# Keeping weight loads and x loads out of the way of the DMA transposes at the start of a fused attention and FFN kernel

## Chip, cores, metric

One core of a Trainium2 chip runs the whole program. The metric is the device time in microseconds (us) of one execution. A profile's span is about 2.3 us shorter than the time of the same execution, so spans are compared with spans and times with times.

## The reference

A pre-norm transformer block in bf16 with 2048 tokens and D = 1024. Attention has 32 query heads of 32 and one shared K and V head. The FFN is 3584 wide.

```python
x = A_x
h = x + attention(layernorm(x), wq, wk, wv, wo)      # 32 heads, one K and one V head
n = layernorm(h)
out = h + (sigmoid(n @ w_gate) * (n @ w_up)) @ w_down
```

## The kernel before

The program is written out by a planner in Python. The planner simulates the engines, fixes the order of instructions on each of them, and adds the waits. On the chip, every engine and every queue then follows its own list in that order. So a wrong guess of a landing time in the planner does not change the result; it leaves an engine waiting.

The start concerns us. x comes in 16 tiles of 128 tokens. VectorE (DVE) normalises each tile in place. Then the tile has to be transposed ("turned") before K, V and Q can be computed from it. Tiles 0 and 1 are turned on TensorE (PE), tiles 2 to 15 by transposing DMAs from SP's queue:

```python
def dma_xT(t):
    xT_ev[t] = dma(lambda: SP.dma_start_transpose(
        out=xnT4[t // 4][:, :, (t % 4) * P:(t % 4 + 1) * P], in_=x_sb[:, t, :]), f"xT{t}", P * D * 5 // 2,
        [xnorm[t]], prio=0, occ=1330.0)
```

The x loads of tiles 8 to 15 go out in pairs from ACT's queue, each after an earlier tile is normalised, and the weight pieces are paced so that the planner's picture of the DMA stays short:

```python
if 1 < ts[-1] < NT - 6:
    load_x([ts[-1] + 5, ts[-1] + 6], [xnorm[ts[-1]]], "act")
# ...
def pump(t):
    while paced and t >= next_piece[0] and pl.dma_free["sp"] < t + (2500.0 if NT - 1 in xT_ev and known([xT_ev[NT - 1]], t) else 600.0):
        # ... issue the next piece of w_o, w_gate, w_up or w_down on SP's queue
```

Scores are computed in "visits" (one pair of exponentials on ACT each). The first 16 visits need K of tiles 0 to 7 only; the following ones need the later tiles. `KNOBS` is a list of planning choices, one tuple for each 8 visits, which a search had picked for this kernel.

The softmax here doesn't subtract the row's maximum and nothing guards it: scores larger than these inputs give would overflow.

## Time and profile before

| | kernel before |
|---|---|
| timed executions | 1083.32 us median of 3 (1081.85 to 1084.2) |
| profiled execution | 1086.84 us, span 1084.6 us |
| ACT busy | 1006.7 us, of it 970.6 us in 1024 exponentials |
| PE busy | 1045.1 us |
| last exponential ends | 1004.06 + 14.97 = 1019.0 us |
| from there to the end | 65.6 us, matmuls |

### The profile page before, as it was taken

The page shows a single profiled execution, that of the slowest core. Times are in us where ns is not written, and L with a number is a line of the kernel's source. Part 1 is how long each engine was busy: PE and PEld are TensorE (multiplying, and loading weights), DVE is VectorE, ACT ScalarE, POOL GpSimd, SP SyncE. Part 2 cuts the span into 40 slices and gives each one's busy share as a digit, 9 for nine tenths or more (in the row PEclk, how much of TensorE's full clock was granted, in tenths as well). Part 3 has the DMA queues.
Part 4 walks back from the last instruction along what each step waited for, and adds up shares of the span by engine and source line. Part 5 has one row for each costly group of instructions (what it writes and reads, how often), then busy time and mean ns, then how long its engine had stood idle before and what let it go on. Part 6 is the DMA issues. An engine that isn't in the chain of part 4 may idle for free.

```text
span 1084.6 us, 31397 instructions
## 1 busy us (share of the span) xinstructions
PE 1045.1 (96%) x12801; PEld 482.2 (44%) x12970; DVE 903.9 (83%) x1757; ACT 1006.7 (93%) x1165; POOL 29.4 (3%) x58
## 2 busy tenths in 40 slices
PE   8899999999999999999999999999999999999998
PEld 6654444444444444444444444444444444444443
DVE  8779989898888889898898989898898989898721
ACT  6889999999999999999999999999999999999610
POOL 2100000000000000000000000000000000000000
PEclk9999999999999999999999999999999999999999
DMA  9986698956969496979569498977959596976994
GB/s 226 229 268 209 178 266 222 268 140 187 261 153 276 128 226 159 258 206 281 157 144 251 140 252 166 248 205 190 251 136 245 143 275 161 238 190 166 270 272 114
DMA packets 309359, 226.60 MB, mean 209 GB/s; under 512 B 121824, under 2 KB 300512, under 8 KB 309216
## 3 DMA queue, kind: packets, MB, share of 16 engines
q1 hardware_dynamic: 306048, 222.37, 80.0%
q10 hardware_dynamic: 3168, 2.23, 0.8%
q8 instruction: 102, 1.67, 0.6%
q14 instruction: 41, 0.34, 0.1%
HBM read 194.12 MB, written 7.86 MB: 186 GB/s over the span
## 4 chain that ended last, share of the span: by engine, by line
PE 65%; ACT 19%; DVE 7%; issue 6%; DMA 2%; POOL 0%; DVEq 0%
PE F_ps L401 54%; ACT Pr L693 17%; PE S_ps L401 11%; DVE Ts L727 2%; ACT tnh L968 2%; DMA zone<-ring 1%; DVE st L338 1%; DVE st L340 1%; DVE Rc L786 1%; DMA ring<-in_B_w_gate_dram 0%; DMA hact<-hst 0%; DVE ring L385 0%; DVE hact L286 0%; DVE ring L378 0%; DMA ring<-in_A_x_dram 0%
## 5 line engine op out<-in xcount | busy, mean ns | idle before, releaser
L693 ACT ACTIVATE Pr<-S_ps 128x1024 bf16<-128x1024 f32 x1024 | 970.6, 1180 | 8.9 <-PE S_ps L401 8.8
L727 DVE TENSOR_TENSOR Ts<-Ts,Pr 128x1024 bf16<-128x1024 bf16 x736 | 481.0, 677 | 33.8 <-ACT Pr L693 31.3
L401 PE MATMUL F_ps<-ring,hnT 128*128 128x512 bf16 (+1 forms) x2032 | 413.1, 380 | 14.1 <-issue 9.7
L401 PEld LDWEIGHTS F_ps<-ring,hnT 128*128 128x128 bf16 (+1 forms) x2116 | 153.4, 97 | 193.0 <-issue 48.1
L401 PE MATMUL F_ps<-zone,hact 128*128 128x512 bf16 (+1 forms) x1136 | 212.0, 380 | 9.0 <-issue 7.9
L401 PE MATMUL S_ps<-QTb,kT 32*128 32x256 bf16 x4096 | 208.3, 273 | 0.3
L401 PEld LDWEIGHTS S_ps<-QTb,kT 32*128 32x128 bf16 x4096 | 64.3, 92 | 208.3 <-ACT Pr L693 144.6
L401 PE MATMUL F_ps<-Pr,Vb 128*32 128x256 bf16 x4096 | 135.3, 274 | 0.0
L968 ACT ACTIVATE tnh<-F_ps 128x512 f32<-128x512 f32 x112 | 84.4, 753 | 43.5 <-PE F_ps L401 43.3
L401 PEld LDWEIGHTS F_ps<-zone,hact 128*128 128x128 bf16 (+1 forms) x1199 | 80.4, 97 | 93.0 <-issue 21.7
L727 DVE TENSOR_TENSOR Ts<-Pr 128x1024 bf16<-128x1024 bf16 x128 | 86.7, 683 | 35.5 <-ACT Pr L693 35.1
L972 DVE SCALAR_TENSOR_TENSOR hst<-tnh,F_ps 128x512 bf16<-128x512 f32 x112 | 76.6, 683 | 46.3 <-PE F_ps L401 39.5
L401 PEld LDWEIGHTS F_ps<-Pr,Vb 128*32 128x32 bf16 x4096 | 97.6, 96 | 30.0 <-issue 18.0
L401 PE MATMUL F_ps<-zone 128*128 128x256 bf16 (+4 forms) x642 | 75.3, 272 | 8.6 <-DMA zone<-ring 3.8
L401 PE MATMUL F_ps<-wo_sb,OT 128*128 128x512 bf16 (+1 forms) x282 | 61.6, 380 | 2.3 <-issue 1.9
L401 PEld LDWEIGHTS F_ps<-zone 128*128 128x128 bf16 (+1 forms) x649 | 43.7, 98 | 31.5 <-issue 11.7
L734 DVE TENSOR_TENSOR Ts<-Ts 128x1024 bf16<-128x1024 bf16 x64 | 44.0, 687 | 1.4
L1002 DVE SCALAR_TENSOR_TENSOR h_sb<-F_ps,h_sb 128x512 bf16<-128x512 f32 x32 | 21.8, 680 | 22.7 <-PE F_ps L401 22.5
L352 POOL TENSOR_SCALAR zb<-mvb 128x1 bf16<-128x1 bf16 (+1 forms) x25 | 10.4, 417 | 1000.6 <-DVE mvb L348 1000.6
L401 PEld LDWEIGHTS F_ps<-wo_sb,OT 128*128 128x128 bf16 (+1 forms) x295 | 22.3, 97 | 28.6 <-issue 7.0
L771 DVE COPY Oc<-F_ps 128x256 f32<-128x256 f32 x60 | 25.1, 419 | 8.5 <-PE F_ps L401 7.4
L776 DVE TENSOR_TENSOR Oc<-F_ps,Oc 128x256 f32<-128x256 f32 x60 | 25.3, 422 | 4.5 <-PE F_ps L401 2.4
(60 smaller groups left out, 330.1 us busy)
## 6 DMA issues: line engine op xcount, KB each, us to landing
ring<-in_B_w_gate_dram SPq DMA_DIRECT2D x314, 256.0 KB, 4.5
ring<-in_B_w_up_dram SPq DMA_DIRECT2D x310, 256.0 KB, 4.7
zone<-in_B_w_down_dram SPq DMA_DIRECT2D x28, 256.0 KB, 4.2
h_sb<-in_A_x_dram SPq DMA_DIRECT2D x16, 256.0 KB, 3.8
out_dram<-h_sb SPq DMA_DIRECT2D x32, 128.0 KB, 3.0
QTb<-q_scratch SPq DMA_DIRECT2D x14, 256.0 KB, 4.5
Pr<-in_B_w_up_dram SPq DMA_DIRECT2D x14, 256.0 KB, 4.9
Pr<-in_B_w_gate_dram SPq DMA_DIRECT2D x12, 256.0 KB, 4.6
```

The costliest lines, as they stand in the source:

```text
L338: a = pl.op("dve", lambda k=k, src=src: DVE.bn_stats(st[:, k, 0, :], src[:, 0:512]), dep, prio=prio, occ=590, lat=756, order=[st_user.get(k)])
L340: b = pl.op("dve", lambda k=k, src=src: DVE.bn_stats(st[:, k, 1, :], src[:, 512:1024]), dep, prio=prio, occ=590, lat=756, order=[st_user.g ...
L401: fn = lambda: PE.matmul(o, lhsT=l, rhs=r, start=start, stop=stop, **kw)
L693: exps[u] = pl.op("act", lambda slot=slot, pb=pb: ACT.activation(out=pslot(slot).rearrange("p (a b) -> p a b", a=2), in_=S_ps[:, pb:pb + 2 ...
L727: o = pl.op("dve", lambda T=T, a=a, b=b: DVE.tensor_tensor(out=T, in0=a, in1=b, op=ALU.add), deps, prio=4, **t_dve(1024, 1.92))
L734: merge_ev[G] = pl.op("dve", lambda T4=T4: DVE.tensor_tensor(out=T4[:, :, 0, :], in0=T4[:, :, 0, :], in1=T4[:, :, 1, :], op=ALU.add), [sum ...
L771: oc_ev[G] = pl.op("dve", lambda: DVE.tensor_copy(out=Oc[:, :], in_=O), [last, o_ev.get(G - 1)], prio=0, **t_dve(256))
L776: a = pl.op("dve", lambda: DVE.tensor_tensor(out=Oc[:, :], in0=O, in1=Ob, op=ALU.add), [last, oc_ev[G], o_ev.get(G - 1)], prio=0, **t_dve( ...
L786: c = pl.op("dve", lambda: DVE.transpose(out=Rc[:, :], in_=R), [last, o_ev.get(G - 1)], prio=0, **t_dve(256))
L968: tanh_of[n] = pl.op("act", lambda: ACT.activation(out=tnh[:, n % 2, :], in_=F_ps[:, b, :], func=ACTF.Tanh, scale=0.5), [last, tn_user.get ...
L972: e = pl.op("dve", lambda: DVE.scalar_tensor_tensor(out=hst[:, n % NST, :], in0=tnh[:, n % 2, :], scalar=1.0, in1=F_ps[:, b, :], op0=ALU.a ...
L1002: e = pl.op("dve", lambda: DVE.scalar_tensor_tensor(out=h_sb[:, t % 4, sl], in0=F_ps[:, b, :], scalar=0.5, in1=h_sb[:, t % 4, sl], op0=ALU ...
```

## The change

The intent: the turns of x are the transfers on which the start hangs, so nothing else should share the DMA with them. Weights wait until the last turn is planned; x loads leave from SP's queue, behind the turns, instead of from ACT's; the planner assumes 1 us more until a turn has landed; and the order is searched anew under these rules. (A cut part of the diff also gives the planner's x loads of tiles 6 and up a later priority.)

```diff
+XT = 1000.0
...
-            go = max(s + 1400.0, self.dma_free[e])
-            other = self.dma_free["act" if e == "sp" else "sp"]
-            both = max(0.0, min(other - go, o.nbytes / 140.0))
-            self.dma_free[e] = go + both + (o.nbytes - both * 140.0) / 280.0
-            o.end = self.dma_free[e] + 900.0 + (PIECE if o.key.startswith("sl") else 0.0)
+            go = max(s + 1400.0, self.dma_free["sp"])
+            self.dma_free["sp"] = go + o.nbytes / 280.0
+            o.end = self.dma_free["sp"] + 900.0 + (PIECE if o.key.startswith("sl") else XT if o.key.startswith("xT") else 0.0)
...
-    KNOBS = [(0, 6, 0, 2, 2), (0, 4, 1, 4, 2), ...]      # cut: 65 tuples
+    KNOBS = [(4, 6, 0, 0, 2), (4, 7, 1, 0, 2), ...]      # cut: 65 tuples
...
-            while paced and t >= next_piece[0] and pl.dma_free["sp"] < t + (2500.0 if NT - 1 in xT_ev and known([xT_ev[NT - 1]], t) else 600.0):
+            if NT - 1 not in xT_ev or xT_ev[NT - 1].end is None:
+                return
+            while paced and t >= next_piece[0] and pl.dma_free["sp"] < t + 2500.0:
...
-                load_x([ts[-1] + 5, ts[-1] + 6], [xnorm[ts[-1]]], "act")
+                load_x([ts[-1] + 5, ts[-1] + 6], [xnorm[ts[-1]]])
```

## The prediction

> **What bounds the kernel now.** I read the page first, then busy time by stretch, then the waits and the timeline of the first 62 us, then the order of instructions in both programs. The page's groups name the costliest work:
>
> ```profile
> L693 ACT ACTIVATE Pr<-S_ps 128x1024 bf16<-128x1024 f32 x1024 | 970.6, 1180 | 8.9 <-PE S_ps L401 8.8
> L968 ACT ACTIVATE tnh<-F_ps 128x512 f32<-128x512 f32 x112 | 84.4, 753 | 43.5 <-PE F_ps L401 43.3
> ```
>
> The 1024 exponentials on ScalarE (ACT) take 970.6 us of 1084.6 and wait only 8.9 us in the whole run, all for scores from TensorE. The 43.5 us of waiting before the tanh falls after the last exponential. Busy time by stretch says where the 8.9 us lie (columns: length, then busy time of PE, PEld, DVE, ACT, POOL, then granted clock, DMA share, GB/s):
>
> ```profile
> 14.00:62.00 48.00, 41.55 (x699) 30.07 (x697) 34.94 (x102) 38.31 (x51) 5.76 (x12) 0.96 0.96 214
> 62.00:1000.00 938.00, 911.67 (x11379) 408.67 (x11530) 825.68 (x1569) 937.11 (x1071) 18.87 (x30) 1.00 0.80 206
> ```
>
> From 62 to 1000 us ACT is idle for 938.00 - 937.11 = 0.9 us. There the exponential is the limit and nothing about transfers can be won. From the first exponential (14.0 us) to 62 us it is idle for 48.00 - 38.31 = 9.7 us. The last exponential ends at 1019.1 us in the timeline of ACT; the 65.5 us after it are the rest of the matmuls on TensorE. So the time is: start to 14.0, ACT's work, ACT's idle time of about 10.6 us, a tail of 65.5 us. The largest gap, in the timeline of ACT:
>
> ```profile
> 52.58 3.83 ACT L693 ACTIVATE Pr<-S_ps 128x1024 bf16<-128x1024 f32 x4 [0.25 <-PE S_ps L401]
> 60.12 1.94 ACT L693 ACTIVATE Pr<-S_ps 128x1024 bf16<-128x1024 f32 x2 [3.71 <-PE S_ps L401]
> ```
>
> ACT runs dry at 56.4. Its scores stand in TensorE's order behind the K and V of the last two token tiles, and the chain that ended last shows what these wait for:
>
> ```profile
> 50.34 1.75 PE F_ps L401 x61
> 52.09 4.85 DMA zone<-ring
> 56.94 0.14 issue
> 57.08 2.44 PE F_ps L401 x25
> ```
>
> That DMA is the transpose ("turn") of tile 15. The timeline of the DMA queue of SP shows that its queue was not free for it:
>
> ```profile
> 43.36 1.86 SPq L600 DMA_DIRECT2D wo_sb<-in_A_wo_dram  x4
> 45.26 3.74 SPq L456 DMA_TRANSPOSE zone<-ring  x2
> ...
> 49.67 3.75 SPq L456 DMA_TRANSPOSE zone<-ring  x2
> ```
>
> Four w_o loads go out just before the turns of tiles 12 and 13, and all later turns follow in the same queue.
>
> **What the Trainium skill says.** "DMA: Bandwidth & Descriptors", section "Issuing engines are not separate DMA queues": transfers started by SP and ACT run on the same 16 DMA engines and interleave. The trace agrees in kind: at 15 to 34 us the ACT-issued x loads and the SP-issued turns share a DMA share of about 0.9 to 1, so moving x loads to SP makes no bandwidth. The same page, "Queues, rings and completion order": on one DMA engine the descriptors of a ring are consumed in ring order. This is the point of the change: an x load behind a turn on SP's ring no longer takes packets from it. No run yet shows it. The same page, "Latency and other measured facts", gives 261 GB/s for a transposing DMA, which is 1.0 us for 256 KB. The trace has a median of 5.2 us from issue to landing (4.1 to 7.0, fourteen turns), and that is what I use.
>
> **The change, part by part.**
>
> (1) Weights after the turns. In the order of SP, before has 8 w_o loads mixed in from tile 8's to tile 15's turns (6 of them ahead of the last turn); after has none until the last turn has been issued. Removed from the time before: 6 x 256 KB = 1.5 MB, about 6 us of transfer at some 270 GB/s, and on SP's queue 1.13 + 0.43 + 1.86 = 3.4 us of issue. Tile 15 is ready at 48.3 us (end of its last scaling on VectorE). Its turn lands at 57.0, 8.7 us later. With a free queue: two turns of 1.3 to 1.9 us of issue each, the second landing 4.1 to 5 us after its own issue, gives 48.3 + 1.5 + 4.5 = 54.3, with up to half a us to spare or to lose. Gain at that wait: about 3 us.
>
> (2) x loads behind the turns. Before, x of tiles 8 to 15 leaves ACT's queue at 15.0, 22.3, 25.4 and 32.6 us. After, each pair stands behind two turns in SP's queue, each of which takes 1.2 to 2.6 us there: I get about 17.5, 25, 30 and 35 us. With 4.8 us to landing (the median of these loads) they arrive at about 22, 29.5, 35 and 40. VectorE takes them up at 21.8, 28.2, 32.6 and 39.2 today. In the new order it scales tiles 8 and 9 before it touches 10, so it has about 0.5 to 1 us more to do before each, but I still expect 0.5 to 2 us of new waiting at three of the four loads, some 3 us in sum, against the 1.2 us it waits today. This is partly paid by VectorE's lighter list: 7 evacuations (5 of q, 1 of K, 1 of V) move from VectorE to ACT, 5 x 0.42 + 0.42 + 0.22 = 2.7 us. So tile 15 is ready at about the same 48 to 49.5 us, and the gain of (1) shrinks by about 0.5 us.
>
> (3) The replanned order. One more pair of exponentials is ahead of the last K and V: 18 score visits (36 exponentials) in TensorE's order instead of 17. That is 1.9 us more of work for ACT to hide the last turn behind. If tile 15 lands at 54 to 55, its K and V and the next scores are through 3.1 us later (57.0 to 60.1 today), at 57.5. ACT then has 36 exponentials at 0.94 us a step (33.8) and 22 evacuations at about 0.27 us (5.9), from 14.0 to 53.7 without idle time, and with some 4 us of the smaller gaps that stay, to 57.7. The 3.7 us gap closes almost wholly, and of the other 6.0 us perhaps 1.5 go, since the earlier turns land sooner as well: 5 us less idle.
>
> (4) Cost on ACT: the 7 evacuations lengthen its list by about 6 x 0.27 + 0.1 = 1.7 us (successive starts in the timeline lie that close, though each lasts 0.39).
>
> (5) The end. The orders of both programs are equal on TensorE for the last 82 rows, from 23 score visits before the last one; on VectorE for the last 90 rows. The tail of 65.5 us is unchanged, and only a shift of the last exponential can show.
>
> (6) The delayed weights. The first w_o matmul is at 101.4 us and the first gate matmul at 120.0; between 95 and 120 us the DMA share is only 0.37. The loads that move out of 32 to 54 us find that room. No cost.
>
> Sum: -5 (idle) + 1.7 (evacuations on ACT) = -3.3 us. 1083.3 - 3.3 = **1080.0 us**.
>
> **Rivals.** *The x loads take the place.* If turns hold SP's queue longer than I think (2.4 us each, as the four slowest), the last x pair arrives at 42 to 43 and tile 15 is ready at 51 to 52; its turn then lands where it does today, and only the extra visit (1.9 us) works against the 1.7 us of evacuations: 1083, or 1085 if the earlier K and V starve ACT too. For it: VectorE already waits once for an x load (1.2 us at 28.2), and SP is one in-order queue where q stores stand as well. Against it: the DMA engines have empty stretches (27 and 25 GB/s at 20 to 22 us). *The turns were slow because of contention.* Then every turn lands in about 4 us once weights and x are out of its way, all K and V come early, and ACT's idle time falls to 2 or 3 us: -7.5 + 1.7, 1077.5. *The delayed weights come back as a wait*: the FFN pieces, held back with w_o, queue against q stores and w_down and the first gate matmuls come late. TensorE would fill in with other work and ACT stay full, so this costs little unless it outlasts 120 us: up to 1086. *The replan itself*: a new order in the first half might leave ACT dry where it now has 0.9 us of idle time in 938; 1 or 2 us either way.
>
> **Range and chances.** All idle time of ACT up to the last exponential is 10.6 us; with 1.7 us of added work even a perfect start ends at about 1074.4. The first rival's worse form is 1085. So 8 in 10: 1075.5 to 1084.5. Two per cent is 21.7 us, twice what the idle time holds, so faster by over 2% is 0.01, slower 0.01, within 0.98.
>
> **What would show it right or wrong.** Right: in the timeline of ACT the 3.7 us gap near 56 us is gone or below 1 us; ACT's busy time in 14 to 62 us rises from 38.3 to about 43; the last exponential ends at about 1016 and the tail after it is 65 to 66 us; the last turn lands at 53.5 to 55. Waits of VectorE for x loads grow from 1.2 to about 3 us. Wrong: a last turn at 57 or later, or VectorE's waits for x above 5 us (the first rival), gaps on ACT after 62 us (replan or weights), or a tail other than 65.5.

## The result, and the profile after

The changed kernel takes 1082.71 us (1082.62 to 1082.78, 4 executions) against 1083.62 us of before (1081.85 to 1084.2, 4 executions, two sessions): ratio 0.9994, 95% interval 0.9977 to 1.0012. A ratio is the mean time of one kernel's fast runs over that of the other's in the same rounds, so it is not quite the ratio of the medians quoted. By the 2% rule the two are the same. Two later sessions, on chips 9 and 2, gave 0.998 (0.9965 to 0.9995) and 0.9983 (0.9967 to 1.0). So, by the medians, the change gains about 0.9 to 2.1 us of the 3.3 predicted, and the prediction's range held. Of the three intervals only the second lies clear of 1.

The two profiles, taken alone, tell a bigger story: the span fell from 1084.6 to 1080.5 us. These are the two groups of the page after:

```profile
L693 ACT ACTIVATE Pr<-S_ps 128x1024 bf16<-128x1024 f32 x1024 | 969.2, 1179 | 4.7 <-PE S_ps L401 4.5
L968 ACT ACTIVATE tnh<-F_ps 128x512 f32<-128x512 f32 x112 | 83.0, 742 | 43.1 <-PE F_ps L401 43.0
```

The exponentials wait 4.7 us in place of 8.9. Busy time by stretch, with the columns as before:

```profile
14.00:62.00 48.00, 45.20 (x742) 33.11 (x740) 37.27 (x100) 42.30 (x61) 5.96 (x12) 0.96 0.91 188
62.00:1000.00 938.00, 911.97 (x11359) 407.60 (x11518) 825.75 (x1569) 938.00 (x1072) 17.62 (x30) 1.00 0.81 209
```

ACT is now idle for 48.00 - 42.30 = 5.7 us before 62 us (9.7 before) and for nothing at all after it. The gap at 56 us is gone. But the timeline of ACT has a new large gap, 12 us earlier:

```profile
40.80 3.77 ACT L693 ACTIVATE Pr<-S_ps 128x1024 bf16<-128x1024 f32 x4 [0.26 <-PE S_ps L401]
47.73 3.97 ACT L693 ACTIVATE Pr<-S_ps 128x1024 bf16<-128x1024 f32 x4 [3.15 <-PE S_ps L401]
```

The chain that ended last, in the same stretch, shows what stood before it:

```profile
35.23 4.08 DMA ring<-in_A_x_dram
39.31 5.47 DMA zone<-ring
44.78 0.14 issue
44.92 2.21 PE F_ps L401 x25
```

The x load of tiles 14 and 15 goes first, the turn of tile 11 lands after it at 44.8 us, and PE stands before K of tiles 10 and 11 although scores of visits that need only tiles 0 to 7 come next in its list. SP's queue in order of time:

```profile
35.23 0.58 SPq L302 DMA_DIRECT2D ring<-in_A_x_dram  x1
35.86 2.02 SPq L583 DMA_DIRECT2D q_scratch<-hact  x4
37.92 2.89 SPq L456 DMA_TRANSPOSE zone<-ring  x2
```

The weights no longer stand between turns, but the x load and four stores of q do. The wait is also handed on to VectorE, whose list has the copy of that K ahead of the normalising of tiles 14 and 15:

```profile
46.95 0.42 DVE L287 CAST kT<-F_ps 128x256 bf16<-128x256 f32 x1 [1.47 <-PE F_ps L401]
...
49.43 0.87 DVE L385 TENSOR_SCALAR ring<-ring,rstd 128x1024 bf16<-128x1024 bf16 x2
```

So tile 15 is ready at 49.43 + 0.87 = 50.3 us in this execution, 2 us later than in the first profile of before (48.3). In two later profiles of the changed kernel (e2, e11) it is ready at 48.5 and 48.4 us.

### The profile page after: what moved, and what is told of

It is laid out like the page before. It is cut to its first block, busy times and chain, and to the rows that moved or that the text cites. A ratio compares the mean times of both kernels' runs of the same rounds, so it can differ in the third digit from the quotient of the medians.

```text
span 1080.5 us, 31405 instructions
## 1 busy us (share of the span) xinstructions
PE 1045.8 (97%) x12803; PEld 483.2 (45%) x12972; DVE 902.7 (84%) x1750; ACT 1007.9 (93%) x1172; POOL 28.4 (3%) x58
## 3 DMA queue, kind: packets, MB, share of 16 engines
q8 instruction: 102, 1.67, 0.7%
## 4 chain that ended last, share of the span: by engine, by line
PE 77%; ACT 11%; DVE 5%; issue 5%; DMA 2%; SPq 0%; POOL 0%; DVEq 0%; ACTq 0%
PE F_ps L401 64%; PE S_ps L401 13%; ACT Pr L693 9%; DVE Ts L727 2%; DMA ring<-in_A_x_dram 1%; ACT tnh L968 1%; DVE st L338 1%; DVE st L340 1%; DMA zone<-ring 1%; DVE Rc L786 0%; DVE ring L385 0%; DVE hst L972 0%; DVE hact L287 0%; DVE Ts L734 0%; DVE ring L378 0%
## 5 line engine op out<-in xcount | busy, mean ns | idle before, releaser
L401 PE MATMUL F_ps<-zone 128*128 128x256 bf16 (+5 forms) x639 | 74.9, 271 | 4.7 <-DMA zone<-ring 2.4
```

Source lines behind the costliest of these rows:

```text
L401: fn = lambda: PE.matmul(o, lhsT=l, rhs=r, start=start, stop=stop, **kw)
```

## The experiments

The questions: why two profiles differ by 4.1 us where the medians differ by 1 or 2; which part of the change gains; and which costs. To move loads without moving anything else, most edits touch the finished lists after planning, so that the orders of PE, VectorE and ACT stay as they were. All runs gave correct results, and each call's kernels share one chip and its runs of before (three calls: e1 to e4, e5 to e8, e9 to e12).

**e1: the kernel before, once more.** No edit.

> The kernel before, unchanged, run again with a profile. Theory A (the profiled execution of before was a long one: 1086.84 us against 1081.85 to 1084.2 in the timed ones, so its gap of 3.7 us is larger than the usual one): times spread over 2 us or more, and this profile's ACT idle time from 14 to 62 us follows its own time, nearer 6 to 8 us than 9.7 if the time is near 1083.5. Theory B (the profiled execution is typical and the 3 us were lost elsewhere in the timed runs of after): every profile of before shows about 9.7 us of idle time there.

Measured: 1082.46 us median (1081.35 to 1085.55, 6 executions); the 11 shared runs of before ran from 1081.92 to 1086.44. The profile fell on an execution of 1081.76 us, 5.1 us shorter than the first profile, of the same program:

```profile
14.00:62.00 48.00, 45.03 (x757) 32.95 (x749) 39.51 (x110) 42.49 (x56) 5.80 (x13) 1.00 0.96 223
```

```profile
49.81 1.94 ACT L693 ACTIVATE Pr<-S_ps 128x1024 bf16<-128x1024 f32 x2 [0.45 <-PE S_ps L401]
52.01 10.28 ACT L693 ACTIVATE Pr<-S_ps 128x1024 bf16<-128x1024 f32 x11 [0.25 <-PE S_ps L401]
```

ACT is idle for 5.5 us instead of 9.7, and the gap of 3.7 us before 60 us, on which the prediction was built, is not there at all. Theory A holds: that gap belongs to some executions of the kernel and not to all.

**e2: the changed kernel, once more.** No edit.

> The changed kernel, unchanged, run again beside the same runs of before. Both theories: 1082.5 to 1083. Theory A: a spread below 0.5 us and ACT idle 5.7 us in 14 to 62 us again, since no load from a second queue runs beside the turns; ratio to before 0.998 to 1.000.

Measured: 1081.32 us (1080.64 to 1082.87, 6 executions), ratio 0.998 (0.9965 to 0.9995). ACT's gap near 45 us was 1.65 us here and its idle time 4.2 us, so both it and the time are less than expected. The spread is 2.2 us and not below 0.5, so the four equal times of the first session were no property of the kernel; it is still about half that of before (4.5 us over 11 runs).

**e3: before, only the w_o loads moved behind the last turn.**

```diff
         lists = pl.lists
+        sp = lists["sp"]
+        cut = max(i for i, o in enumerate(sp) if o.key and o.key.startswith("xT")) + 1
+        wo = [o for o in sp[:cut] if o.key and o.key.startswith("wo")]
+        lists["sp"] = [o for o in sp[:cut] if o not in wo] + wo + sp[cut:]
```

> Before, with only the six w_o loads moved behind the last turn in SP's queue; the orders of TensorE, VectorE and ACT are before's. Theory C (the weights between the turns held the turns up): the last turn lands 2 to 3 us sooner (about 54) and the time falls by 1.5 to 3 us. Theory D (VectorE and TensorE's own order set the start, the weights fit into gaps): the last turn lands within 1 us of before and the time within 1 us.

Measured: 1081.49 us (1079.24 to 1083.07), ratio 0.9979 (0.9963 to 0.9996), so about -2.3 us. The turns of tiles 14 and 15 leave SP's queue from 46.70 us, against 49.67 in the first profile of before and 48.90 in e1; the median from issue to landing of a turn is 3.9 us against 5.2 and 4.8. The last turn leaves at 48.0 us and has landed by 52.0. Theory C holds, though the interval is wide (0.4 to 4.0 us): this one move gives as much as the whole change (e2, 0.998).

**e4: before, only the x loads moved behind the turns.**

```diff
-            eng = ACT if ring == "act" else SP
+            eng = SP
...
+        for t in (3, 5, 7, 9):
+            x = next(o for o in lists["act"] if o.key == f"x{t + 5}")
+            lists["act"].remove(x)
+            x.eng = "sp"
+            at = next(i for i, o in enumerate(lists["sp"]) if o.key == f"xT{t}")
+            lists["sp"].insert(at + 1, x)
```

> Before, with only the four x loads of tiles 8 to 15 moved from ACT's queue to SP's, each pair behind two turns; all other orders are before's. If the x loads behind turns cost VectorE time: its waits for x grow from 1.2 to 3 us or more, the last turn lands 1 to 3 us later, time +1 to +2 us. If two queues at once were what made before vary: the spread of its times falls below 0.5 us, with the time about the same.

Measured: 1085.0 us (1083.06 to 1086.71), ratio 1.0016 (0.9999 to 1.0033), so about +1.7 us, with an interval that just reaches 1. The spread did not fall. VectorE's waits for x grew to 3.5 us. The last turn landed at about 54.7 us, earlier than in the first profile of before (56.9) and less than 1.5 us after that of e1 (53.7 to 54.0): the loss lies earlier, not there. How 1.1 us of such a wait becomes 3.8 us on ACT is seen in three timelines of this run, of VectorE, PE and ACT:

```profile
34.87 0.69 DVE L338 BATCH_NORM_STATS2 st<-ring 128x6 f32<-128x512 bf16 x1 [1.10 <-DMA ring<-in_A_x_dram]
...
36.15 0.41 DVE L286 CAST hact<-F_ps 128x256 bf16<-128x256 f32 x1
```

```profile
36.61 1.25 PE L401 MATMUL F_ps<-zone 128*128 128x256 bf16 x8 [2.88 <-DVE hact L286]
```

```profile
38.89 1.94 ACT L693 ACTIVATE Pr<-S_ps 128x1024 bf16<-128x1024 f32 x2 [3.77 <-PE S_ps L401]
```

VectorE stands before the x of tile 12; a q evacuation is behind that in its list; PE waits for the bank that this evacuation frees, and the next scores stand behind PE's wait. PE's granted clock is also 0.50 from 37.4 to 40.7 us, so those scores come slowly (more on this after e12).

**e5: before with both moves,** the edits of e3 and e4 together.

> Before with both moves of loads (w_o behind the last turn, x behind the turns on SP), all other orders before's. If the two effects add: -2.3 us of w_o and +1.7 us of x give about -0.6 us against before (ratio 0.999 to 1.000). What then separates it from the changed kernel is the replanned order alone: if the replan is worth what the prediction said (an extra pair of exponentials ahead of the last K and V, and more evacuations on ACT), the changed kernel is 1 to 2 us faster than this one.

Measured: 1084.2 us (1081.73 to 1085.6), ratio 1.0005 (0.9989 to 1.0021). The gain of e3 and the loss of e4 cancel, as the sum said. The changed kernel has these two moves and a new order, and lies at 0.998 to 0.9994; so the new order seems worth 1.2 to 2.7 us with these loads, though the intervals overlap and they come from different calls.

**e6: the changed kernel with six w_o loads back among the turns.** The waits of these loads were dropped, which is safe because nothing else uses their tile yet. They stand before the turns of tiles 10, 11 and 12 (one, one and four); in before they stand before those of 8, 10 and 12.

```diff
+        wo = [o for o in lists["sp"] if o.key and o.key.startswith("wo")][:6]
+        for o in wo:
+            lists["sp"].remove(o)
+            o.deps = []
+        for t, some in ((10, wo[:1]), (11, wo[1:2]), (12, wo[2:])):
+            at = next(i for i, o in enumerate(lists["sp"]) if o.key == f"xT{t}")
+            lists["sp"][at:at] = some
```

> The changed kernel with six w_o loads put back among the turns in SP's queue where before has them; all other orders are the changed kernel's. If the weights between turns cost the time: 1 to 2.5 us slower than the changed kernel, turns 12 to 15 landing 2 us or more later. If the replanned order hides a late turn (one more visit ahead of the last K and V): within 0.7 us of the changed kernel.

Measured: 1085.28 us (1083.89 to 1085.84), ratio 1.0018 (1.0003 to 1.0033), that is 2.6 to 4 us above the changed kernel's ratios; e7 and e8, which keep w_o behind the turns, ran at 1080.63 and 1081.27 us. The turns of tiles 12 and 13, behind four w_o loads, took 5.2 to 6.3 us to land, against 3.1 to 3.2 in the changed kernel. ACT's largest gap, 2.85 us, is still the one before K of tiles 10 and 11; 0.74 us more come before the scores at 50.4 us. One more visit ahead of the last K and V did not hide that. Part one of the change is confirmed from both sides.

**e7: the changed kernel with x of tiles 8 to 15 on ACT's queue again.**

```diff
-            o = dma(lambda: SP.dma_start(x_sb[...], xf[...]), ...)
+            o = dma(lambda: (ACT if ts[0] > 7 else SP).dma_start(x_sb[...], xf[...]), ...)
...
+        for t in (3, 5, 7, 9):
+            x = next(o for o in lists["sp"] if o.key == f"x{t + 5}")
+            lists["sp"].remove(x)
+            x.eng = "act"
+            at = next(i for i, o in enumerate(lists["act"]) if not o.nbytes and o.end - o.lat >= xnorm[t].end)
+            lists["act"].insert(at, x)
```

> The changed kernel with the x loads of tiles 8 to 15 issued from ACT's queue again; all other orders are the changed kernel's. If x behind the turns costs about 1.7 us as in the run on before: about 1079.5, 1 to 2 us faster than the changed kernel and so faster than both, with VectorE's waits for x below 1 us. If the turns of tiles 10 and 11 suffer from sharing the DMA engines: the same time, the wait of K and V of tiles 10 and 11 still there.

Measured: 1080.63 us (1079.75 to 1081.11, 5 executions), ratio 0.9975 (0.996 to 0.9989). The new gap near 45 us is gone. Only the gap before the second K was longer, 2.39 us.

**e8: the changed kernel with one score visit ahead of K and V of tiles 10 and 11.**

```diff
+        pe = lists["pe"]
+        s12 = [o for o in pe if o.tag == ("S", 12)]
+        end = pe.index(s12[0])
+        start = max(i for i, o in enumerate(pe) if o.tag == ("S", 11)) + 1
+        kv = next(i for i in range(start, end) if xT_ev[10] in pe[i].deps or xT_ev[11] in pe[i].deps)
+        for o in s12:
+            pe.remove(o)
+        pe[kv:kv] = s12
```

> The changed kernel with one score visit moved ahead of K and V of tiles 10 and 11 in TensorE's order, nothing else. If TensorE's fixed order is what turns a late turn into idle time of ACT: the ACT gap of 1.65 to 3.15 us near 45 us falls below 1 us and the time by 1 to 2 us, to about 1080. If the turn of tile 15 sets the end of the start anyway: the gap moves to 57 us and the time stays within 0.7 us.

Measured: 1081.27 us (1080.99 to 1081.59, 5 executions), ratio 0.9982 (0.9968 to 0.9996). ACT's gap is 1.39 us, at 46.4 us, not below 1; in three profiles of the changed kernel it was 3.15, 1.65 and 1.68. The time is within the changed kernel's. No changed kernel ran in this call, so this stays inconclusive: the order of PE may help, but the run does not show it. Its ratio to before, 0.9982, is that of e2 and e11.

**e9: x of tiles 8 and 9 on SP's queue, of 10 to 15 on ACT's.** The edit is e7's, with the condition `ts[0] > 9` and without the first pair.

> The changed kernel with x of tiles 8 and 9 left behind the turns of tiles 2 and 3 on SP's queue, and x of tiles 10 to 15 issued from ACT's queue. If x on a second queue delays the turns it runs beside (the gap of ACT at the second K grew from 1.32 to 2.39 us when all x loads were on ACT's queue): that gap is 1.3 us again, the rest as with all on ACT, and the time 0.5 to 1 us below that run, about 1079.8. If x of tiles 8 and 9 is needed early: VectorE waits for it and the time is that of all on ACT or above.

Measured: 1080.37 us (1079.66 to 1081.64), ratio 0.9965 (0.9947 to 0.9983), the same as e10 beside it. The gap at the second K is 1.32 us in both, so its 2.39 us in e7 was one execution's and no effect of the queue. A miss.

**e10 and e11: e7's kernel and the changed kernel on one chip.**

> The kernel with all x loads of tiles 8 to 15 on ACT's queue once more, beside the others on one chip: 1080 to 1081, 0.7 to 2 us below the changed kernel.

> The changed kernel once more, on the same chip as the two above: 1081.3 to 1082.8, ratio to before 0.997 to 0.9995.

Measured: e10 1080.2 us (1079.84 to 1081.26), ratio 0.9964 (0.9948 to 0.998); e11 1082.48 us (1081.56 to 1083.38), ratio 0.9983 (0.9967 to 1.0). All six executions of e10 are below all six of e11, and the medians differ by 2.3 us. Busy time of e10 by stretch, and its timeline of ACT:

```profile
14.00:62.00 48.00, 47.18 (x799) 34.55 (x795) 39.81 (x107) 45.26 (x65) 6.31 (x13) 1.00 0.87 204
```

```profile
41.38 21.60 ACT L693 ACTIVATE Pr<-S_ps 128x1024 bf16<-128x1024 f32 x23 [0.26 <-PE S_ps L401]
```

ACT never runs dry from 41.4 us on and is idle for 2.7 us in all. The corresponding line of e11 still has a gap:

```profile
46.31 3.77 ACT L693 ACTIVATE Pr<-S_ps 128x1024 bf16<-128x1024 f32 x4 [1.68 <-PE S_ps L401]
```

So e10 beats both kernels: weights behind the turns and the new order, but x loads on the second queue. In these two profiles ACT's idle time (2.7 and 4.1 us) is 1.4 us of a difference of 2.4. The other 1.0 us lies after the last exponential, where PE of e11 waited twice for transfers and PE of e10 did not:

```profile
1034.25 1.89 PE L401 MATMUL F_ps<-ring,hnT 128*128 128x512 bf16 x8 [0.58 <-DMA hnT<-hn]
1055.12 0.61 PE L401 MATMUL F_ps<-ring,hnT 128*128 128x512 bf16 x2 [0.42 <-DMA ring<-in_B_w_up_dram]
```

Whether other executions of e11 have these two waits is not known.

**e12: the changed kernel planned with before's list of choices** (`KNOBS` of before, all else of after).

> The changed kernel's rules (weights after turns, x behind turns, landing margin) but planned with before's list of choices: all 5 evacuations of q stay on VectorE (23 evacuations on ACT against 30). If the new list is needed to live with late x loads: 1 to 3 us slower than the changed kernel, ACT idle above 6 us in 14 to 62. If the rules alone do it: within 0.7 us.

Measured: 1089.75 us (1089.15 to 1093.21), ratio 1.0057 (1.0038 to 1.0075). It is slower by 7 us than e11 and not by 1 to 3. ACT's idle time to 62 us is 6.6 us, as the first theory said; but the last exponential ends only 2.1 us later than in e11 (1015.8 and 1013.7 us), and 71.7 us follow it instead of 66.5. PE was busy for 906.1 us between 62 and 1000 us against 911.9 in e11, and for 67.6 us after the last exponential against 61.7: 6 us of matmuls were not fitted beside the exponentials and remain for the tail. Neither theory had the tail in it.

**A check over the profiles.** If the time is a constant plus ACT's idle time between 14 and 1000 us, the difference must be the same for all kernels with one order of the compute engines (e8 moves one score visit; e12 has another tail and is left out):

| order | profile | time | ACT idle | time - idle |
|---|---|---|---|---|
| before | first | 1086.84 | 10.6 | 1076.3 |
| before | e1 | 1081.76 | 5.7 | 1076.1 |
| before | e3 | 1080.72 | 5.3 | 1075.4 |
| before | e4 | 1083.06 | 7.1 | 1076.0 |
| before | e5 | 1085.02 | 9.2 | 1075.8 |
| after | first | 1082.78 | 5.7 | 1077.1 |
| after | e2 | 1081.27 | 4.2 | 1077.1 |
| after | e6 | 1083.95 | 6.4 | 1077.5 |
| after | e7 | 1081.11 | 3.6 | 1077.5 |
| after | e8 | 1080.99 | 3.9 | 1077.1 |
| after | e9 | 1080.48 | 2.6 | 1077.9 |
| after | e10 | 1080.13 | 2.7 | 1077.4 |
| after | e11 | 1082.49 | 4.1 | 1078.4 |

The differences stay within 0.9 us for before's order and 1.3 us for after's, where e11 stands out by the 1.0 us in its tail. Their means are 1075.9 and 1077.5.

**What I overlooked: PE's granted clock.** In all five profiles with a gap on ACT of 2.8 us or more, or with several of 1.4 us and more (before, after, e4, e5, e6), the granted clock of PE is half for 3.3 us or more at that place. In the other nine it is 1.00 from 14 to 62 us. Busy time of before, of the changed kernel's first profile and of e2, with the columns as before (the clock is the third number from the end):

```profile
57.20:60.60 3.40, 3.40 (x36) 2.13 (x35) 0.65 (x2) 0.48 (x1) 0.00 (x0) 0.50 0.67 205
```

```profile
45.30:48.60 3.30, 3.30 (x36) 2.10 (x35) 1.59 (x6) 0.87 (x1) 0.93 (x2) 0.50 0.76 145
```

```profile
45.30:48.60 3.30, 3.12 (x61) 1.91 (x61) 3.19 (x13) 2.15 (x3) 1.19 (x2) 1.00 0.73 139
```

Each time a stop of PE ends shortly before: 2.49, 2.37, 2.88 and 2.63 us (before, after, e4, e6), and in e5 three stops of 1.67, 0.89 and 0.56 us within 6 us. So a late turn costs ACT its wait, and in such executions also the slow K, V and scores after it. The mean clock listed for each execution tells which ones had it (0.997 or 0.998 instead of 1.00): 16 of before's 39 timed executions with a listed clock, at a mean of 1084.8 us against 1082.8 for the rest; 8 of the changed kernel's 16, at 1082.7 against 1081.6; all of e4 and e6, 4 of e5's 6 and 1 of e12's; none of e3, e7, e8, e9 and e10. Two executions of before at 1.00 took 1085.6 and 1086.4 us, so it is not the only cause of long ones.

## Why the prediction was right or wrong

**The frame was right.** The time is ACT's work, its gaps at the start, and a fixed tail; the table shows it over 13 profiles, to about 1 us. The tail was to be unchanged: 65.6 and 65.2 us in the first two profiles (66.5 in e11). No delayed weight came back as a wait of ACT: in the three profiles of the changed kernel it is idle for 0.0 us from 62 to 1000 us.

**Step (4), the evacuations on ACT, was right.** It said +1.7 us; the two means differ by 1.6 us. Taken without the tail, the stretch from the first to the last exponential less ACT's idle time, the means are 994.0 and 995.5 us. No run moved the evacuations alone, so that they make this difference is inferred.

**The base of the sum was wrong, and this is what made the gain too large.** The prediction took 5 us of idle time out of a profile of 1086.84 us and subtracted the result from a median of 1083.3 us. Within the pair of profiles, the sum is nearly right: idle time from 10.6 to 5.7 us is -4.9 us, where it had said -5. That it fits so well is luck, since step (3) below got the parts wrong. And the usual execution of before has less idle time to lose. With the table's 1075.9, before's median of 1083.44 us (43 executions over all sessions, 1080.47 to 1087.14) means 7.5 us of idle time, and the changed kernel's 1082.48 us (16 executions, 1080.64 to 1083.38) less 1077.5 means 5.0. This is an estimate from those numbers: -2.5 us of idle time, +1.6 us of evacuations, about -1 us. The prediction also took the 3.1 us from the last turn to the next scores as what K, V and scores need; in that profile they ran at half the clock.

**Step (1), the weights, was right in kind and about in size.** It said 3 us at the wait for the last turn. Moving w_o alone gave -2.3 us (e3); putting it back cost 2.6 to 4 us by ratios from different calls (e6).

**Step (2), the x loads, had the waits right and the consequence wrong.** It said some 3 us of VectorE's waiting for x; the profile has 2.6. It then counted only what reaches tile 15, 0.5 us. The runs show 1.7 us lost on before's order (e4, its interval just reaching 1) and 2.3 us on after's (e10 against e11; 1.4 of it is ACT's idle time in the two profiles). What was missing is that a wait in one fixed list blocks whatever stands behind it: PE before K of tiles 10 and 11 in the changed kernel, and VectorE before an evacuation that PE needs in e4. The rival "the x loads take the place" was the right one, at about the size of its milder form, but acting in the middle of the start and not at the last turn.

**Step (3) was half right.** The gap at 56 us closed. The other gaps were to fall from 6.0 to about 4.5 us; they fell to 2.6 us, and the new one of 3.15 us came in their place. The last turn was expected at 53.5 to 55 us. In the first profile after, it left at 52.3 us and took between 3.2 and 4.3 us, so it landed at 55.5 to 56.6 us, because tile 15 was ready 2 us later; no wait on it shows. That is the execution with the slow clock near 46 us. In e2 and e11, without it, the last turn left at 50.6 and 50.3 us and landed between 53.5 and 54.5 us, as expected.

**The Skill's points.** That moving loads between issuing queues makes no bandwidth (the Trainium skill, "DMA: Bandwidth & Descriptors", section "Issuing engines are not separate DMA queues") agrees with the runs: the DMA share in 14 to 62 us is 0.92 in e11 and 0.87 in e10, and the faster one has the lower. What moves is the order in which things land. The prediction's inference that an x load behind a turn takes no packets from it has some support: the median from issue to landing of a turn is 3.9 us in e4 against 4.8 in e1, and 3.4 in e11 against 4.6 in e10. But the turns and x loads then leave later, and that weighs more.

**What stays open.** Why one execution of before has the gap at the last turn and the next does not is settled in part: the one has the stop of 2.49 us and the slow clock after it, the other neither, but what lets its last turn leave 2 us earlier (50.2 and 52.1 us) is not known. That a second queue beside the turns causes the spread is not supported: e4 and e5, with all loads on SP, spread over 3.7 and 3.9 us. The worth of the new order by itself rests on a comparison across calls. That the slow clock is caused by the stop before it was not tested by a run of its own.

## What to carry to other kernels

Before subtracting a gap from a median, check that the profiled execution is a usual one; where its time lies outside the timed ones, profile again, since a gap can belong to the execution and not to the kernel. Clear a critical transfer's queue of what is needed late (here w_o, loaded from 32 us on and first used at 101 us), but do not put behind it what is needed soon: the x loads were better off in a second queue, at 1080.2 against 1082.5 us. Where every engine follows a fixed list, cost a late transfer by what stands behind the instruction that waits for it, not by the wait alone, and look at PE's granted clock after the wait.

## What the Trainium skill lacked or had wrong

- "DMA: Bandwidth & Descriptors", section "Issuing engines are not separate DMA queues": it says that several issuing engines save only the sequencer's time. The queue decided 2.3 us (e10 1080.2, e11 1082.5 us) with no more bandwidth, because a load on its own queue need not be issued behind transposes that wait for their input. The page doesn't name this.
- The same page, "Latency and other measured facts": from its 261 GB/s one gets an estimate of 1.0 us for a transpose of 256 KB. The runs show 3.0 us as the least from issue to landing, 3.4 to 5.2 us as medians of the profiles, and 1.2 to 2.7 us on SP's queue for the issue alone, once 3.8. For a transpose of this size on this chip, no page gives an issue time by which a queue of fourteen can be planned; the same page's cycle counts for "previous generations" are for other sizes.
- "TensorE: Matmul & The Clock Gate", section "Part 1: The HAM clock gate (the "warmup" mystery)": it gives an idle window of about 3.4 us, free-running, before the clock falls. Here shorter stops of PE were followed by a granted clock of 0.50: after 2.37 us (changed kernel) from 45.3 to 48.6 us, after 2.49 us (before) from 57.2 to 60.6, after 2.63 us (e6) from 46.7 to 50.0, after 2.88 us (e4) from 37.4 to 40.7; after 1.45 and 1.78 us (e2, e11) it stayed at 1.00.
- No page has that executions of one unchanged kernel of one core differ by 5 us through gaps at the start: 1081.76 and 1086.84 us, with ACT idle for 5.7 and 10.6 us. The slow clock of the point above is in the second and not in the first.
